# Normalised rows stored once, in the order in which the sequence transform reads them

## The chip, the cores and the metric

The kernel runs on one core of a Trainium2 chip. The metric is the device time of one execution in microseconds (us): 886.37 us before the change, the median of two runs (886.31 and 886.42).

## The reference

The input x has 2048 rows of 640 floats. Each row is normalised (mean and variance over its 640 values), and the output is the sum of x, a Fourier mixing of the normalised rows, and a two-layer network with a hidden width of 1536. Everything is float32.

```python
xn = layernorm(x)                                # no scale, no shift
a, b = xn @ dft_hid_re.T, xn @ dft_hid_im.T      # 640 x 640
y = dft_seq_re @ a - dft_seq_im @ b              # 2048 x 2048
h = gelu_tanh(xn @ w1 + b1)                      # 640 -> 1536
return x + y + (h @ w2 + b2)                     # 1536 -> 640
```

## The kernel before

Every matmul takes a float32 operand as two rounded halves ("high" on ACT, then "low" = value minus high on DVE, lines 187 and 190) and is done as three products (lines 312 to 314, or 332). So an operand is ready for PE only when an ACT and a DVE instruction have run for it, and both engines take their instructions strictly in the order of the program, as do the two queues that issue DMAs, SP and POOL. A DMA on SP also waits until the DMA issued eight places earlier on SP has landed, and POOL's DMAs likewise among themselves: each queue cycles through eight completion semaphores.

The rows are worked in four blocks of 512 rows (128 row chunks 0 to 15, four to a block). The program has these stages, all written out in one order by hand:

- **Block 0, the loop over i.** Block 0's hidden layer, twelve units of 128 columns: `hidden(g)` makes unit g (15 matmuls), `gelu` puts it through the activation and the split into `hs`, `output(g)` multiplies it into five PSUM banks. The weights come through `load_w1`, `load_w2` and are split by `prep_w1`, `prep_w2` three and one steps ahead. `background(i)` normalises the blocks 0, 1 ("a") and 2 ("b") meanwhile: `ln_stats` (two BN_STATS and a BN_AGGR a chunk), `ln_scale` (a square root on ACT, for which ACT changes its function table and back, and five tiny DVE instructions), `ln_apply` (one DVE instruction a chunk, in place). `put_z` regroups the normalised rows of a block into a tile `z` by 16 small DMAs on POOL, and `make_forms` transposes and splits `z` into the forms that the pairs stage multiplies. `z_a` goes into the tile `row`, and `z_b` into its own.
- **Pairs, k = 0 to 5.** The hidden layers of blocks 1 and 2 together. In each pair two units of block 1 (a1, a2) are used at once, and two of block 2 (b1, b2) are stored in DRAM (`keep`, tensor `gs`) and read back later. Units live in the two buffers `ab`; `zc` is a temporary in the buffers `zt`; `w2r` is a ring of three buffers. `beside_pair` adds block 0's sums to x (`finish`) and prepares the hidden transform's matrices.
- **Steps p = 0 to 13.** `output` of block 2's stored units, 15 matmuls a step. `between(p)` adds block 1's sums to x: `finish(1, e)` adds the bias on ACT, transposes bank e on DVE (line 395), and adds it on DVE to `xo[1]` (line 397), which is loaded from DRAM into the place `xab2` by four DMAs on SP (line 388). Block 2's sums use the banks 5, 6, 7, 3 and 4, so that step 2 needs the banks 3 and 4 of block 1 emptied. `between` also normalises block 3 and puts it into `z3`; from step 7 on `z3` is transposed and split for block 3's hidden layer, and the weights of that layer are split anew (`prep_w1`, loaded by `load_w1`).
- **Block 3, then the sequence transform.** Block 3's hidden layer runs beside `build`, which reads the normalised rows back from the DRAM tensor `xn`. The rest of the program, from about 350 us on, is the sequence transform.

The normalised rows go to DRAM twice: `put_rows(c)` stores a chunk in `xs` as it stands (four DMAs a block on POOL), and `by_chunks(t)` later copies a block from `xs` into `xn` in the order in which `build` reads it, by one DMA on SP inside DRAM.

Of the kernel before, what the change touches and what calls it, by code (L numbers as in the profile page):

```python
# [15 lines left out]
P = 128  # L16
# [10 lines left out]
def kernel(  # L27
# [66 lines left out]

    dram = ctx.enter_context(tc.tile_pool(name="dram", bufs=1, space=bass.MemoryType.DRAM))

    xs = dram.tile([S, D], F32, name="xs")
    xn = dram.tile([NS, P, D], F32, name="xn")

    gs = dram.tile([NF, P, TB], F32, name="gs")  # L100
# [98 lines left out]
    def rows_of(ap, t):  # L199
        return ap[t * TB : (t + 1) * TB].rearrange("(n r) d -> r n d", r=B)  # L200
# [29 lines left out]
    def ln_apply(c, eng=nc.vector, put=True):  # L230
        m = MV[:, slot[c]]
        eng.tensor_scalar(xt[c], xt[c], m[:, 0:1], m[:, 3:4], op0=ALU.subtract, op1=ALU.mult)  # L232
        if put:
            put_rows(c)

    def put_rows(c):
        nc.gpsimd.dma_start(xs[c * P : (c + 1) * P], xt[c])

    def ln_apply_chunked(dst, c, j0=0, j1=ND):

# [22 lines left out]
    def load_z(z, t):  # L263

        v = rows_of(xs, t)
        for q in range(Q):
            nc.gpsimd.dma_start(z[q * B : (q + 1) * B], v[:, :, q * DQ : (q + 1) * DQ])

    def transpose_z(key, z, j):
        zt[key] = mr.tile([P, TB], F32, tag="zt", bufs=2, name=f"zt{key}")  # L270
# [63 lines left out]
            )  # L334
        return acc

    def term(g, acc):

        a = mr.tile([P, TB], F32, tag="ab", bufs=2, name=f"ab{g}")
        nc.scalar.activation(a, acc, AF.Copy)  # L340
        return a

# [399 lines left out]
    def put_z(z, rows):  # L742

        for a in range(NC):
            for q in range(Q):
# [2 lines left out]
                    rows[a * B : (a + 1) * B, :, q * DQ : (q + 1) * DQ],  # L748
                )

    def background(i):

        if i == 0:
            for c in range(NC):
                ln_apply(c)
            A["rows_a"] = rows_in("rt2")
            for c in range(NC, 2 * NC):
                load_x(c, home=A["rows_a"])
            for c in range(2 * NC, 3 * NC):
                ln_stats(c)  # L760
        if i == 1:
            ln_scale(NC)
            Z["b"] = zo_tile("z_b")
            for c in range(2 * NC, 3 * NC):
                ln_apply(c, put=False)
            put_z(Z["b"], A["rows_b"])
            for c in range(2 * NC, 3 * NC):
                put_rows(c)
            ln_stats(NC)
            ln_stats(NC + 1)  # L770
        if i == 2:
            ln_stats(NC + 2)
            ln_stats(NC + 3)
            ln_scale(NC)
            Z["a"] = as_z(row_places)
            for c in range(NC, 2 * NC):
                ln_apply(c, put=False)
            put_z(Z["a"], A["rows_a"])
            for c in range(NC, 2 * NC):
                put_rows(c)  # L780
        if i == 4:
            open_place(*PLACES[7])
            new_forms(0, "vb", "ua", "va")
            make_forms("b", "vb0", "vb1", "ob0")
        if i == 5:
            make_forms("a", "ua0", "ua1", "va0")
        if i == 6:
            new_forms(3, "t1")
            make_forms("a", "oa0", "va1")
        if i >= 6:  # L790
            (ua, va), (ub, vb) = ((Z[k][:, :, : 2 * B], Z[k][:, :, 2 * B : 4 * B]) for k in "ab")
        if i == 6:
            add(ub, ub, ua, ALU.subtract)
        if i == 7:
            open_place(*PLACES[8])
            make_forms("b", "t10", "t11")
            add(vb, vb, ub, ALU.subtract)
        if i == 8:
            turn_x("t20", "b")
            turn_x("t21", "b")  # L800
            add(ua, vb, ua, ALU.subtract)
            add(va, va, vb, ALU.subtract)
            load_xo(0)


    XF = {}
# [96 lines left out]
        for e in es:  # L903
            add_block(xo[t], e, oacc[t][e], f"ot{t}_{e}", eng, bias=b2c[:, e : e + 1], **(home or {}))

    def by_chunks(t):

        nc.sync.dma_start(xn[:, t * B : (t + 1) * B], xs[t * TB : (t + 1) * TB].rearrange("(n r) d -> n r d", r=B))

    def store_sums(t, *ks):  # L910
        for k in ks or range(len(YCOLS)):
# [7 lines left out]
    def beside_pair(k, at):  # L919

        if k == 0:
            if at == 5:
                make_forms("a", "t30", "t31")
            if at == 6:
                make_forms("a", "t40", "t41")
                load_w(0, 0)
                load_w(1, 0)
            if at == 4:
                finish(0, 0, 1)
                store_sums(0, 0)  # L930
            return
        j = k - 1
        if k == 1:
            if at == 2:
                finish(0, 2, home=in_zt)
            if at == 5:
                finish(0, 3, home=in_zt)
                store_sums(0, 1)
                finish(0, 4)
                store_sums(0, 2)  # L940
        if at == 6:
            if k < NT:
                by_chunks(k - 1)
# [39 lines left out]
    def pair(k):  # L983
# [16 lines left out]
        beside_pair(k, 5)  # L1000
        put_out(0 if k else 3)
        window(x_, "C", 0, "t2", False)
        v = term(b1_, x_)
        beside_pair(k, 6)
        put_out(3 if k else 0)
        window(z_, "C", 2, "vb", False, ("C", 4, "ob0"))
# [21 lines left out]
    def between(p):  # L1028
# [2 lines left out]
            ln_stats(12)  # L1031
            ln_stats(13)
        if p == 1:
            finish(1, 3, 4, home=in_zt, eng=nc.vector)
            ln_stats(14)
        if p == 2:
            ln_stats(15)
            ln_scale(NC)
            Z["z"] = zo_tile("z3")
            for c in range(3 * NC, 4 * NC):  # L1040
                ln_apply(c, put=False)
            put_z(Z["z"], row_places)
            for c in range(3 * NC, 4 * NC):
                put_rows(c)
# [47 lines left out]
    for i in range(NF - 2):  # L1092
# [11 lines left out]
        gelu(i + 2, acc)  # L1104
        output(i)
    make_pieces(0, "Bh", "Bl", "+", "Dh", "Dl", "Ch", "Cl")
    split_x("t20")
# [570 lines left out]
```

## Time and profile before

| | |
|---|---|
| median of the runs | 886.37 us |
| the profiled execution, its own time | 887.41 us |
| its span, first to last instruction | 885.6 us |
| PE busy | 852.0 us, 96% of the span |
| DVE, ACT, POOL busy | 77%, 41%, 10% |
| mean granted TensorE clock | 0.986 |

Times below are microseconds from the start of the span. In a row of the timeline stand: start, length, engine, line, operation, tiles, shape, how many, and in brackets how long the engine had been idle before it and what ended that. In a row of waits stand: who waited, for what, the total, how many times, and the longest.

### The profile page before, as it was taken

To read this page: it belongs to the slowest core of one execution; us is meant where nothing else is said; L and a number is where in the kernel's file an instruction comes from. 1 tells how busy PE (TensorE), PEld (TensorE's weight loads), DVE (VectorE), ACT (ScalarE), POOL (GpSimd) and SP (SyncE) were. 2 spreads that over 40 slices of the span, in tenths; PEclk is the share of its full clock that TensorE was granted. 3 is DMA by queue.
4 is the path that set the end of the run, shared out by engine and by line. 5 is a ranking of instruction groups with operands and counts; after the bars stand their busy time and mean duration, and the time that the engine had idled before them with its cause. 6 is when DMAs were issued, how large, how long until landed. Compare 5 with 4: busy or idle time off the path is not lost.

```text
span 885.6 us, 10569 instructions
## 1 busy us (share of the span) xinstructions
PE 852.0 (96%) x3711; PEld 700.2 (79%) x3711; DVE 686.2 (77%) x897; ACT 367.3 (41%) x528; POOL 90.1 (10%) x142
## 2 busy tenths in 40 slices
PE   8997988999498999999999999999999999999997
PEld 7776877888386888888888888888888888888885
DVE  6859786876474377897989888888977988886587
ACT  6546554655144455543333444332222432323241
POOL 0370043333060500000000000000000000000000
PEclk9998999999699999999999999999999999999999
DMA  7893568988888787795964349947476679904364
GB/s 231 247 283 117 110 169 262 296 249 281 198 241 206 187 313 276 144 189 146 206 133 147 83 132 320 271 88 187 114 168 200 209 218 221 338 19 172 119 162 105
DMA packets 201188, 171.77 MB, mean 194 GB/s; under 512 B 65808, under 2 KB 172560, under 8 KB 200496
## 3 DMA queue, kind: packets, MB, share of 16 engines
q1 hardware_dynamic: 187168, 142.13, 60.5%
q0 software_dynamic: 8688, 28.06, 9.3%
q10 hardware_dynamic: 5280, 0.92, 0.5%
q8 instruction: 29, 0.48, 0.2%
q14 instruction: 23, 0.19, 0.1%
HBM read 120.99 MB, written 51.38 MB: 195 GB/s over the span
## 4 chain that ended last, share of the span: by engine, by line
PE 77%; DMA 7%; issue 6%; DVE 5%; ACT 1%; SPq 1%; POOL 1%; DVEq 0%; ACTq 0%; POOLq 0%
PE banks L312 24%; PE banks L313 24%; PE banks L314 24%; PE banks L332 5%; DMA w1r<-in_B_w_dram 2%; DMA z_b<-r 1%; DMA xab<-in_A_x_dram 1%; SPq L290 1%; POOL z L746 1%; DMA xs<-r 1%; DMA row<-rt 1%; DMA w2r<-in_B_w_dram 1%; DVE w1f L190 1%; DVE st L216 1%; DVE row L232 0%
## 5 line engine op out<-in xcount | busy, mean ns | idle before, releaser
L313 PE MATMUL banks<-as,xab 128*128 128x512 f32 x407 | 158.3, 389 | 0.0
L312 PE MATMUL banks<-as,xab 128*128 128x512 f32 x407 | 158.3, 389 | 0.0
L314 PE MATMUL banks<-as,xab 128*128 128x512 f32 x407 | 158.3, 389 | 0.0
L187 ACT ACTIVATE as<-r 128x1024 fp32r<-128x1024 f32 x80 | 85.0, 1062 | 173.6 <-PE banks L314 148.8
L190 DVE TENSOR_TENSOR as<-r,as 128x1024 fp32r<-128x1024 f32 x80 | 97.1, 1215 | 39.1 <-ACT as L187 39.1
L314 PEld LDWEIGHTS banks<-as,xab 128*128 128x128 f32 x407 | 76.4, 188 | 16.0
L313 PEld LDWEIGHTS banks<-as,xab 128*128 128x128 f32 x407 | 76.4, 188 | 15.9
L312 PEld LDWEIGHTS banks<-as,xab 128*128 128x128 f32 x407 | 76.4, 188 | 15.8
L312 PE MATMUL banks<-as,xc 128*128 128x512 f32 x224 | 87.1, 389 | 0.0
L313 PE MATMUL banks<-as,xc 128*128 128x512 f32 x224 | 87.1, 389 | 0.0
L314 PE MATMUL banks<-as,xc 128*128 128x512 f32 x224 | 87.1, 389 | 0.0
L187 ACT ACTIVATE as<-rt 128x1024 fp32r<-128x1024 f32 x32 | 34.0, 1063 | 69.8 <-PE banks L314 57.9
L312 PE MATMUL banks<-hs,xc 128*128 128x512 f32 x120 | 47.9, 399 | 12.9 <-DVE ot L395 12.9
L332 PE MATMUL banks<-xt,xab 128*128 128x512 f32 x240 | 57.6, 392 | 0.6 <-DVE xab L190 0.6
L190 DVE TENSOR_TENSOR hs<-ab,hs 128x512 fp32r<-128x512 f32 x36 | 26.3, 730 | 37.8 <-ACT hs L187 37.8
L332 PEld LDWEIGHTS banks<-xt,xab 128*128 128x128 f32 x240 | 44.6, 188 | 11.3 <-DVE xab L190 1.9
L314 PEld LDWEIGHTS banks<-as,xc 128*128 128x128 f32 x224 | 42.0, 188 | 8.8
L313 PEld LDWEIGHTS banks<-as,xc 128*128 128x128 f32 x224 | 42.0, 188 | 8.7
L312 PEld LDWEIGHTS banks<-as,xc 128*128 128x128 f32 x224 | 42.0, 188 | 8.7
L313 PE MATMUL banks<-hs,xc 128*128 128x512 f32 x120 | 47.7, 397 | 0.0
L314 PE MATMUL banks<-hs,xc 128*128 128x512 f32 x120 | 47.6, 397 | 0.0
L190 DVE TENSOR_TENSOR as<-rt,as 128x1024 fp32r<-128x1024 f32 x32 | 38.7, 1210 | 5.3 <-ACT as L187 5.3
(221 smaller groups left out, 1671.2 us busy)
## 6 DMA issues: line engine op xcount, KB each, us to landing
raw<-in_A_dft_seq_re_dram SPq DMA_DIRECT2D x64, 256.0 KB, 5.6
raw<-in_A_dft_seq_im_dram SPq DMA_DIRECT2D x64, 256.0 KB, 5.3
w1r<-in_B_w_dram SPq DMA_DIRECT2D x144, 80.0 KB, 3.1
wit<-wst POOLq DMA_DIRECT2D x15, 384.0 KB, 4.3
ws<-wit SPq DMA_DIRECT2D x15, 384.0 KB, 4.4
xn<-xs SPq DMA_DIRECT2D x4, 1280.0 KB, 7.6
wit<-wst POOLq DMA_DIRECT2D x20, 256.0 KB, 4.3
forms_ab<-xab SPq DMA_DIRECT2D x4, 1280.0 KB, 7.5
```

The lines of the kernel that those rows point to most:

```text
L187: nc.scalar.activation(h, s, AF.Copy)
L190: nc.vector.tensor_tensor(l, s, h.bitcast(F32), op=ALU.subtract)
L216: nc.vector.bn_stats(st[:, h, :], xt[c][:, h * half : (h + 1) * half])
L290: eng.dma_start(t[q * B : (q + 1) * B], v[q, :, :, f0 : f0 + P])
L312: nc.tensor.matmul(acc, wh, mh, start=first, stop=False, skip_group_check=goes_on)
L313: nc.tensor.matmul(acc, wh, ml, start=False, stop=False, skip_group_check=goes_on)
L314: nc.tensor.matmul(acc, wl, mh, start=False, stop=last, skip_group_check=goes_on)
L332: nc.tensor.matmul(acc, W1[i][:, a, j * P : (j + 1) * P], XT[j][:, b], start=n == 0, stop=n == len(steps) - 1)
L746: nc.gpsimd.dma_start(z[q * B : (q + 1) * B].rearrange("r (c a) d -> r a c d", a=NC)[:, a], rows[a * B : (a + 1) * B, :, q * DQ : (q + 1) ...
```

## The change

`xs` and the four copies inside DRAM are gone. `put_rows(t, rows)` stores a block straight into `xn`, by four DMAs of 32 partitions each. Block 2's four go out on SP, the others on POOL. `background` and the new `late` spread the row statistics and the square roots otherwise over the first steps; in `pair`, unit b1 gets a buffer of `w2r` (but in the last pair) and unit b2 is made in place in `zc`, so that neither is in `ab`; in `between`, the banks 3 and 4 of block 1 are transposed into `ab` in step 1 and added to `xo[1]` in step 4, and block 3 is normalised in step 3 instead of 2.

```diff
-    xs = dram.tile([S, D], F32, name="xs")
...
-    def put_rows(c):
-        nc.gpsimd.dma_start(xs[c * P : (c + 1) * P], xt[c])
...
-    def term(g, acc):
-        a = mr.tile([P, TB], F32, tag="ab", bufs=2, name=f"ab{g}")
+    def term(g, acc, a=None):
+        if a is None:
+            a = mr.tile([P, TB], F32, tag="ab", bufs=2, name=f"ab{g}")
...
+    def put_rows(t, rows, eng=nc.gpsimd):
+        for a in range(NC):
+            eng.dma_start(
+                xn[:, t * B : (t + 1) * B].rearrange("(c a) r d -> a r c d", a=NC)[a], rows[a * B : (a + 1) * B]
+            )
...
     def background(i):
         if i == 0:
             for c in range(NC):
                 ln_apply(c)
+            put_rows(0, row_places)
             A["rows_a"] = rows_in("rt2")
             for c in range(NC, 2 * NC):
                 load_x(c, home=A["rows_a"])
-            for c in range(2 * NC, 3 * NC):
-                ln_stats(c)
-        if i == 1:
-            ln_scale(NC)
-            Z["b"] = zo_tile("z_b")
-            for c in range(2 * NC, 3 * NC):
-                ln_apply(c, put=False)
-            put_z(Z["b"], A["rows_b"])
-            for c in range(2 * NC, 3 * NC):
-                put_rows(c)
-            ln_stats(NC)
-            ln_stats(NC + 1)
+            ln_stats(8)
+            ln_stats(9)
         if i == 2:
-            ln_stats(NC + 2)
-            ln_stats(NC + 3)
+            put_rows(2, A["rows_b"], nc.sync)
+            ln_stats(4)
+            ln_stats(5)
+        if i == 3:
             ln_scale(NC)
             Z["a"] = as_z(row_places)
             for c in range(NC, 2 * NC):
-                ln_apply(c, put=False)
+                ln_apply(c)
             put_z(Z["a"], A["rows_a"])
-            for c in range(NC, 2 * NC):
-                put_rows(c)
+            put_rows(1, A["rows_a"])
...
+    def late(i):                # called behind gelu(i + 2), ahead of output(i)
+        if i == 0:
+            ln_stats(10)
+            ln_stats(11)
+        if i == 1:
+            ln_scale(NC)
+            Z["b"] = zo_tile("z_b")
+            for c in range(2 * NC, 3 * NC):
+                ln_apply(c)
+            put_z(Z["b"], A["rows_b"])
+        if i == 2:
+            ln_stats(6)
+            ln_stats(7)
...
-    def by_chunks(t):
-        nc.sync.dma_start(xn[:, t * B : (t + 1) * B], xs[t * TB : (t + 1) * TB].rearrange("(n r) d -> n r d", r=B))
+    def turn_sum(t, e):
+        nc.scalar.activation(oacc[t][e], oacc[t][e], AF.Identity, bias=b2c[:, e : e + 1])
+        yt = mr.tile([P, TB], F32, tag="ab", bufs=2, name=f"ot{t}_{e}")
+        nc.vector.transpose(yt, oacc[t][e])
+        return yt
...
-        v = term(b1_, x_)
+        v = term(b1_, x_, None if k == LASTK else early.tile([P, TB], F32, tag="w2r", bufs=3, name=f"v{k}"))
...
-        keep(b2_, unit(b2_, x_, zc))
+        keep(b2_, unit(b2_, x_, zc, zc))
...
     def between(p):
         if p == 1:
-            finish(1, 3, 4, home=in_zt, eng=nc.vector)
+            held = [turn_sum(1, e) for e in (3, 4)]
+            A["held"] = held
             ln_stats(14)
         if p == 2:
             ln_stats(15)
+        if p == 3:
             ln_scale(NC)
             Z["z"] = zo_tile("z3")
             for c in range(3 * NC, 4 * NC):
-                ln_apply(c, put=False)
+                ln_apply(c)
             put_z(Z["z"], row_places)
-            for c in range(3 * NC, 4 * NC):
-                put_rows(c)
+            put_rows(3, row_places)
             new_xt(3)
+        if p == 4:
+            for e, yt in zip((3, 4), A["held"]):
+                d = xo[1][:, :, e * B : (e + 1) * B]
+                add(d, d, yt.rearrange("p (n i) -> p n i", i=B))
         if 4 <= p < 7:
-            finish(1, p - 4, eng=nc.vector)
-        if p == 5:
-            by_chunks(3)
+            finish(1, p - 4, home=in_zt, eng=nc.vector)
```

**The queues of the first 70 us.** On POOL stand, before, the stores of a block (line 237) and the 16 regrouping DMAs of a `z` (line 746) by turns; `row` holds block 0's rows and later `z_a`, `r` block 2's and `rt` block 1's.

```order
L237 DMA xs<-row 128x640 x4
L746 DMA z_b<-r_241 32x4x160 x16
L237 DMA xs<-r_241 128x640 x4
L746 DMA row<-rt_332 32x4x160 x16
L237 DMA xs<-rt_332 128x640 x4
L899 DMA gs<-ab_1028 128x512
L899 DMA gs<-ab_1064 128x512
```

In the changed kernel the same queue reads so (line 743 is the new store, 735 the regrouping, 902 `keep`):

```order
L743 DMA xn<-row 32x4x640 x4
L735 DMA z_b<-r_240 32x4x160 x16
L735 DMA row<-rt_331 32x4x160 x16
L743 DMA xn<-rt_331 32x4x640 x4
L902 DMA gs<-v_1027 128x512
L902 DMA gs<-zc_999 128x512
```

Block 2's store has left POOL from between the two regroupings. It stands on SP now, between the weight loads of the steps i = 2 and i = 3:

```order
L278 DMA w1r_460<-in_B_w_dram 32x5x128 x4
L285 DMA w2r_465<-in_B_w_dram 128x640
L743 DMA xn<-r_240 32x4x640 x4
L278 DMA w1r_522<-in_B_w_dram 32x5x128 x4
L285 DMA w2r_527<-in_B_w_dram 128x640
L278 DMA w1r_598<-in_B_w_dram 32x5x128 x4
```

The loads behind it on SP are moved back by four DMAs.

**DVE, the steps p = 1 and 2.** Before (`ot` is a transposed bank, `xab` here the place of `xo[1]`, `g` a stored unit read back, `row` block 3's rows):

```order
L190 TENSOR_TENSOR hs_2066<-g_1866,hs_2066 128x512
L395 STREAM_TRANSPOSE ot_3_2072<-banks 128x512
L397 TENSOR_TENSOR xab_2010<-xab_2010,ot_3_2072 128x16x32
L395 STREAM_TRANSPOSE ot_4_2076<-banks 128x512
L397 TENSOR_TENSOR xab_2010<-xab_2010,ot_4_2076 128x16x32
L216 BN_STATS st_91<-row 128x6 x2
L217 BN_AGGR mv<-st_91 128x2
L190 TENSOR_TENSOR hs_2097<-g_1868,hs_2097 128x512
```

In the changed kernel, the steps 1 to 3 on DVE begin so:

```order
L189 TENSOR_TENSOR hs_2056<-g_1857,hs_2056 128x512
L912 STREAM_TRANSPOSE ot_3_2062<-banks 128x512
L912 STREAM_TRANSPOSE ot_4_2065<-banks 128x512
L215 BN_STATS st_90<-row 128x6 x2
L216 BN_AGGR mv<-st_90 128x2
L189 TENSOR_TENSOR hs_2085<-g_1859,hs_2085 128x512
L215 BN_STATS st_91<-row 128x6 x2
L216 BN_AGGR mv<-st_91 128x2
L189 TENSOR_TENSOR hs_2108<-xab_1966,hs_2108 128x512
```

and the steps 3 and 4, behind the square root's five small instructions, go on so:

```order
L231 TENSOR_SCALAR row<-row,mv 128x640 x4
L189 TENSOR_TENSOR hs_2158<-xab_1966,hs_2158 128x512
L463 TENSOR_TENSOR xab_2000<-xab_2000,ot_3_2062 128x16x32
L463 TENSOR_TENSOR xab_2000<-xab_2000,ot_4_2065 128x16x32
L384 STREAM_TRANSPOSE ot_0_2164<-banks 128x512
L386 TENSOR_TENSOR xab_2000<-xab_2000,ot_0_2164 128x16x32
```

The addition of bank 3 no longer stands between the transposes of the banks 3 and 4; both additions come behind the normalisation of block 3 and the split of unit 28.

More of the change, by code (lines that the diff above doesn't have):

```diff
@@ L228, in ln_scale, with ln_apply @@
         nc.vector.scalar_tensor_tensor(r, t, 1.5, r, op0=ALU.add, op1=ALU.mult)
-    def ln_apply(c, eng=nc.vector, put=True):
+    def ln_apply(c, eng=nc.vector):
         m = MV[:, slot[c]]
         eng.tensor_scalar(xt[c], xt[c], m[:, 0:1], m[:, 3:4], op0=ALU.subtract, op1=ALU.mult)
-        if put:
-            put_rows(c)
-    def put_rows(c):
-        nc.gpsimd.dma_start(xs[c * P : (c + 1) * P], xt[c])
     def ln_apply_chunked(dst, c, j0=0, j1=ND):
@@ L261, in zo_tile @@
         return out_pool.tile(list(shape), dtype, tag="zo", bufs=1, name=name)
[L263 to L267, printed above, removed]
     def transpose_z(key, z, j):
@@ L941, in beside_pair @@
         if at == 6:
-            if k < NT:
-                by_chunks(k - 1)
             turn_w(0, j)
@@ L1040, in between @@
             for c in range(3 * NC, 4 * NC):
-                ln_apply(c, put=False)
+                ln_apply(c)
             put_z(Z["z"], row_places)
-            for c in range(3 * NC, 4 * NC):
-                put_rows(c)
+            put_rows(3, row_places)
             new_xt(3)
+        if p == 4:
+            for e, yt in zip((3, 4), A["held"]):
+                d = xo[1][:, :, e * B : (e + 1) * B]
+                add(d, d, yt.rearrange("p (n i) -> p n i", i=B))
         if 4 <= p < 7:
-            finish(1, p - 4, eng=nc.vector)
-        if p == 5:
-            by_chunks(3)
+            finish(1, p - 4, home=in_zt, eng=nc.vector)
         for j in {7: (0,), 8: (1, 2), 9: (3, 4)}.get(p, ()):
@@ L1104 @@
         gelu(i + 2, acc)
+        late(i)
         output(i)
```

## The prediction, as it was made before the changed kernel ran

> **What bounds the kernel now.** I read the page's shares first, then what PE waited for, then PE's timeline at each of those waits.
>
> ```profile
> PE 852.0 (96%) x3711; PEld 700.2 (79%) x3711; DVE 686.2 (77%) x897; ACT 367.3 (41%) x528; POOL 90.1 (10%) x142
> PEclk9998999999699999999999999999999999999999
> PE 77%; DMA 7%; issue 6%; DVE 5%; ACT 1%; SPq 1%; POOL 1%; DVEq 0%; ACTq 0%; POOLq 0%
> ```
>
> PE is the bound: 96% busy, and the chain that ended last is 77% PE. The 13% of DMA, "issue" and others in the chain is what a change of transfers and orders can reach; no matmul is taken away here. The waits of PE:
>
> ```profile
> PE banks L312 <- DVE ot L395: 12.9, 2, 11.2
> PE banks L332 <- ACT as L187: 4.6, 1, 4.6
> ```
>
> These are the two largest; the next two (on ACT's `hs` and `zc`) stand in brackets in the rows below. All four lie in the first 277 us, and behind them PE runs without a gap. A wait costs more than its length where the clock falls afterwards, so I price each place by the matmuls' starts:
>
> ```profile
> 67.68 0.39 PE L314 MATMUL banks<-hs,r 128*128 128x512 f32 x1
> 72.64 6.44 PE L332 MATMUL banks<-xt,as 128*128 128x512 f32 x15 [4.58 <-ACT as L187]
> 78.92 0.40 PE L312 MATMUL banks<-hs,r 128*128 128x512 f32 x1
> 82.33 3.56 PE L332 MATMUL banks<-xt,as 128*128 128x512 f32 x15
> 148.49 0.50 PE L312 MATMUL banks<-xab,w1f 128*128 128x512 f32 x1 [2.36 <-ACT zc L187]
> 225.52 0.39 PE L314 MATMUL banks<-hs,xc 128*128 128x512 f32 x1
> 237.09 0.79 PE L312 MATMUL banks<-hs,xc 128*128 128x512 f32 x1 [11.18 <-DVE ot L395]
> 242.37 0.42 PE L312 MATMUL banks<-hs,xc 128*128 128x512 f32 x1
> 267.37 0.39 PE L314 MATMUL banks<-hs,r 128*128 128x512 f32 x1
> 271.31 0.49 PE L312 MATMUL banks<-hs,rt 128*128 128x512 f32 x1 [3.55 <-ACT hs L187]
> 276.69 0.39 PE L313 MATMUL banks<-hs,rt 128*128 128x512 f32 x1
> ```
>
> At full clock the 15 matmuls from 78.92 to 82.33 take 3.41, 0.227 each. So: **A**, 67.68 to 78.92 holds 16 matmuls (3.63) and lasts 11.24: 7.6 lost. **B**, 225.52 to 242.37 holds 13 (2.95) and lasts 16.85: 13.9 lost. **C**, 267.37 to 276.69 holds 14 (3.18) and lasts 9.32: 6.1 lost. After 2.36 idle the next matmul is near its full speed (0.50 against 0.39); after 4.58, 15 of them take 6.44 instead of 3.56, so 2.9 of A's 7.6 is a slow clock, and after 3.55 there is a slow stretch too.
>
> [...]
>
> **B: the two banks, line by line.** Bank 3's addition waits on DVE for `xo[1]`, and bank 4's transpose stands behind it.
>
> ```profile
> 219.65 5.70 SPq L388 DMA_DIRECT2D xab<-in_A_x_dram  x4
> DMA to landing us min/median/max: 10.4/11.0/11.2
> 223.40 0.71 DVE L395 STREAM_TRANSPOSE ot<-banks 128x512 f32<-128x512 f32 x1
> 235.71 0.69 DVE L397 TENSOR_TENSOR xab<-xab,ot 128x512 f32<-128x512 f32 x1 [11.60 <-DMA w1r<-in_B_w_dram]
> 236.32 0.71 DVE L395 STREAM_TRANSPOSE ot<-banks 128x512 f32<-128x512 f32 x1
> 246.66 0.82 DVE L190 TENSOR_TENSOR xab<-w1r,xab 128x640 fp32r<-128x640 f32 x1
> ```
>
> The second line is of the four loads of `xo[1]`: the last, issued at about 224.4, lands at about 235.4, so I read the addition's wait as one for it, though the row names a weight load that landed beside it. With both transposes side by side bank 4 is empty at 223.40 + 2 x 0.71 = 224.8, ahead of PE, which asks for it at 225.52 + 0.23. All **13.9** goes.
>
> What is late next? With bank 4's three matmuls done at 226.4, PE's steps then begin at 226.4 + 3.41 x (p - 3). The additions still wait for 235.4, now in step 4, and queued behind them on DVE is the split of unit 29: 235.4 + two additions 1.38 + transpose 0.71 + addition 0.69 + a weight split 0.82 (last row) + the split itself 0.69 = 239.7. PE begins unit 29 (step 7) at 240.0 and reads the low half one matmul later. That just fits; each microsecond by which `xo[1]` comes later is paid from there on.
>
> **C: the copy on SP.** The weight loads of block 3 stand on SP behind `xn<-xs`, which waits for `xs` to land:
>
> ```profile
> SPq L908 <- DMA xs<-row: 9.3, 1, 9.3
> 259.35 11.73 SPq L290 DMA_DIRECT2D w1r<-in_B_w_dram  x12
> 270.00 0.74 ACT L187 ACTIVATE as<-w1r 128x640 fp32r<-128x640 f32 x1 [9.69 <-DMA w1r<-in_B_w_dram]
> ```
>
> ACT waits 9.7 for such a load at 270.00, the unit's split stands behind it, and PE pays 6.1. The copy is removed, so the loads go out when their buffers come free. But block 3's `z3` is made a step later, and PE arrives 14 sooner:
>
> ```profile
> 218.61 0.94 SPq L209 DMA_DIRECT2D row<-in_A_x_dram  x2
> DMA to landing us min/median/max: 4.9/6.9/10.0
> 239.27 0.88 DVE L216 BATCH_NORM_STATS2 st<-row 128x6 f32<-128x320 f32 x2
> 241.58 2.18 DVE L232 TENSOR_SCALAR row<-row,mv 128x640 f32<-128x640 f32 x4
> 255.47 1.30 DVE L271 STREAM_TRANSPOSE ztx<-z 128x512 f32<-128x512 f32 x2
> 258.32 0.69 DVE L190 TENSOR_TENSOR hs<-g,hs 128x512 fp32r<-128x512 f32 x1
> ```
>
> The last chunk of x lands at the latest at 219.0 + 10.0 = 229.0 (second line: the loads of block 3's chunks). From its statistics to the end of the normalisation were 243.76 - 239.27 = 4.5, and one unit's split (0.69) now stands between: 234.2. From there to the first transpose of `z3` 255.47 - 243.76 = 11.7: 245.9. Unit 32's split ended 3.5 behind that transpose: 249.4, and PE wants it in step 10, at 226.4 + 7 x 3.41 = 250.3. There is 0.9 to spare, and the next two units, each with two more transposes or splits ahead of it, have less. While `z3` comes in, four weight loads, the store of block 3's rows and that of block 1's sums share the engines with it. I take 1.2 for new waits here, from bounds of 0 and 6.1 (the wait as it was), nearer to nothing because the steps fit by the rows. C gives 6.1 - 1.2 = **4.9**.
>
> **A: `z_a` comes late.** ACT's weight split stands behind the forms of `z_a`, and these behind 16 DMAs on POOL.
>
> ```profile
> 34.48 2.18 DVE L232 TENSOR_SCALAR r<-r,mv 128x640 f32<-128x640 f32 x4
> 67.22 1.30 DVE L271 STREAM_TRANSPOSE ztua<-row 128x512 f32<-128x512 f32 x2 [7.86 <-DMA xs<-rt]
> 37.39 4.37 POOL L746 DMA_DIRECT2D z_b<-r  x8 [8.55 <-DVE r L232]
> 49.69 2.17 POOL L237 DMA_DIRECT2D xs<-r  x4 [1.42 <-DMA z_b<-r]
> 57.86 3.80 POOL L746 DMA_DIRECT2D row<-rt  x7 [0.41 <-DMA xs<-r]
> 62.35 1.09 POOL L746 DMA_DIRECT2D row<-rt  x2 [0.68 <-DMA row<-rt]
> ```
>
> With eight DMAs in flight at most, two halves of `z_b` take 49.69 - 37.39 = 12.3, or 6.15 a half. In the new order one more split (0.69) stands ahead of block 2's normalisation, so `z_b` starts at 38.1, and `z_a` can follow at 50.4, where `xs<-r` stood. Its second half goes out 6.15 later, at 56.5, the last of it at 56.5 + 7 x 0.55 = 60.4; before, the last went out at 62.9 and the transpose followed at 67.22, 4.3 later. So the transpose comes at 64.7, 2.5 sooner, and PE's matmuls at 70.1 instead of 72.64. PE has been ready since 67.9: 2.2 idle, and no slow stretch. At 70.1 + 3.41 = 73.5 it stands where it stood at 78.92: **5.4** gained. Bounds: all 7.6, and -0.7, where `z_a` lands no sooner for leaving POOL's line and the 0.69 is paid.
>
> A store of 32 partitions in 2560-byte pieces is in no row. The 128-partition store of the same bytes went from 49.69 to 57.86 (when POOL's wait for its last part ended): 8.2; the same bytes in `z_b`'s pieces of 640 took 12.3. I take the first, since its pieces are of 2560 bytes too; the other end and beyond is a rival below. On SP the four stand ahead of the weight loads from unit 9 on. Were these held until 57.86, as POOL was, they would still go out 12 before PE wants unit 9 at 70.1, so I cost that at nothing; without that cover, A's wait would be for the weights. The statistics and roots of blocks 1 and 2 are the same instructions in other places. What they delay on ACT and DVE are units that PE wants two steps later, 30 matmuls or 6.8 a step; if that cover is gone, `z_a` is later by as much, as with the 0.69.
>
> [...]
>
> ```profile
> q0 software_dynamic: 421, 0.92, 60.0%
> q1 hardware_dynamic: 673, 0.56, 44.0%
> ```
>
> **The pairs.** Unit a2 waited for the store of b1 to leave `ab`, and no longer does:
>
> ```profile
> ACT ab L351 <- DMA gs<-ab: 5.5, 2, 3.4
> ```
>
> The PE wait that follows is the 2.36 at 148.49. I take 0.7 of it, between nothing and 2.4, near nothing, because DVE's additions in that chain keep their places. The new places (`zc` held until its store lands, `w2r` used once more a pair) are reused a pair later, against waits of 3.4 at most for such a store; I cost them at nothing, and if that cover were gone it would be that wait again.
>
> **The sum.** 13.9 + 4.9 + 5.4 + 0.7 = 24.9 off the profiled execution's 887.41 is 862.5; the median of the runs lies 1.04 below that execution, so **861.5**. PE has no gap behind 277 us, and the engines' order is unchanged there, so nothing is given back.
>
> **The rivals.** *The engines are the limit* (0.22): with shares that sum to over 100%, `z_a` needs the same bytes moved as before, lands at 67.9, and A gives -0.7. The sum is 18.8, the time 867.6. Against it: the loads of SP that share the engines at that time are not wanted until later, and the store now stands among them. *The steps do not fit* (0.16): `z3`, `xo[1]` or the weight loads land 2 to 4 later when crowded into 14 fewer microseconds, and C keeps its 6.1 and B gives 10: 24.9 - 4.9 - 3.9 = 16.1, 870.3. *All waits go* (0.05): 30.0 off, 856.4. *Slower* (0.03): the 32-partition stores use the engines badly. Each block's store then adds d to the two regroupings in flight, `z_a` comes 2d later, and A's 5.4 turns into a loss of 2d - 5.4, with a slow clock's 2.9 on top. From d = 11 us, 1.31 MB in 19 instead of 8.2, the whole change is a loss (24.9 - 2 x 11 - 2.9 = 0); at d = 13 the time is 890. Against it: even the pieces of 640 bytes took 12.3. *It does not do what it says* falls away: the order has the transposes side by side and no copy. My forecast, 857 to 866, keeps 0.54.
>
> Range for 8 in 10: 856 to 872, from all waits gone to the steps not fitting with a little spread; without that rival too much would be left out. A change of 2%, 17.7 us, is about what a measurement of this kernel tells from none. Faster than 868.6 are the forecast (0.54), all waits gone (0.05), most of the engines' limit (0.16 of 0.22, as 867.6 is close to the mark) and a little of the steps (0.02): 0.77. Slower by that much is 0.02, the rest 0.21.
>
> **What would show it.** B: no wait of PE for a transposed bank, and DVE's wait for `xo[1]` moved behind block 3's normalisation. C: no ACT wait of 9 for a weight load; any wait of PE between 235 and 262 is the new one. A: the transpose of `z_a` at about 64.7 and the next 15 matmuls in 3.4; if it stays at 67, the engines were the limit. I am wrong if PE waits longer than 3.4 anywhere behind 80 us.

## The result, and the profile after the change

864.17 us, the median of two runs (863.83 and 864.51), against 886.37: a ratio of 0.975 with an interval of 0.9708 to 0.9792. Beside other kernels the changed one ran again, 866.60 in the median of three executions (865.85 to 866.72) against 888.82, a ratio of 0.9745 (0.9726 to 0.9763). A fourth of these executions, at 4900.77, stands outside everything and is not read. The kernel before took 888.2 to 888.8 in all later comparisons, so times are compared as ratios. The profiled execution took 864.51, 22.9 less than the one before; the spans, 862.5 and 885.6, differ by 23.1.

The shares and the chain on the page:

```profile
PE 846.3 (98%) x3711; PEld 696.1 (81%) x3711; DVE 686.9 (80%) x897; ACT 366.7 (43%) x528; POOL 87.2 (10%) x138
PE 74%; DMA 11%; DVE 6%; ACT 3%; SPq 2%; issue 2%; POOL 1%; POOLq 0%; DVEq 0%; ACTq 0%
```

The largest waits of PE, but for the first one of the span (total, times, longest):

```profile
PE banks L681 <- DVE xp L236: 2.2, 1, 2.2
PE banks L300 <- DVE ot L384: 2.2, 2, 1.7
PE banks L320 <- ACT as L186: 1.9, 2, 1.6
PE banks L300 <- ACT zc L186: 1.6, 2, 1.3
```

The work is the same (3711 matmuls); the waits of 12.9 for `ot` and 4.6 for `as` at the top of the list have become 2.2 and 1.9. Of the 12.9, 11.2 stood at B; the other 1.7, a wait for a transposed bank of block 0 in pair 1, was there before and is there after. Where the time came from is read by comparing the start of the same matmul in both traces:

| stretch | gained, us | the changed kernel is ahead by |
|---|---|---|
| start of the span to the first `output` (22.17, now 23.00) | -0.8 | -0.8 |
| to 54 us | 1.5 | 0.7 |
| place A (78.92, now 75.56) | 2.7 | 3.4 |
| pairs (148.49, now 143.50) | 1.6 | 5.0 |
| place B (242.37, now 223.43) | 13.9 | 18.9 |
| place C (276.69, now 252.31) | 5.4 | 24.4 |
| the rest, to the last matmul (879.46, now 856.46) | -1.4 | 23.0 |

The largest part, B's 13.9, comes from the order of the two transposes in step 1 and does not need the rows to be stored once; the new store bears on C and A.

**B.** PE's matmuls, then DVE:

```profile
220.48 0.39 PE L302 MATMUL banks<-hs,xc 128*128 128x512 f32 x1
220.71 0.39 PE L300 MATMUL banks<-hs,xc 128*128 128x512 f32 x1
218.31 1.31 DVE L912 STREAM_TRANSPOSE ot<-banks 128x512 f32<-128x512 f32 x2
229.72 1.29 DVE L463 TENSOR_TENSOR xab<-xab,ot 128x512 f32<-128x512 f32 x2 [0.71 <-DMA xab<-in_A_x_dram]
```

Where 11.57 lay between two matmuls there are now 0.23. Both transposes are done at 219.6, and the additions, 10 us later, wait 0.71 for `xo[1]`; the wait is on DVE still, where nothing hurries.

**C.** The transpose of `z3` on DVE, an ACT split that waits for its weights, and the two matmuls of PE that come late:

```profile
242.09 1.31 DVE L259 STREAM_TRANSPOSE ztx<-z 128x512 f32<-128x512 f32 x2 [3.00 <-DMA xn<-row]
254.46 0.74 ACT L186 ACTIVATE as<-w1r 128x640 fp32r<-128x640 f32 x1 [2.62 <-DMA w1r<-in_B_w_dram]
245.61 0.50 PE L301 MATMUL banks<-hs,r 128*128 128x512 f32 x1
249.46 0.50 PE L301 MATMUL banks<-hs,rt 128*128 128x512 f32 x1
```

No copy stands ahead of the weight loads; ACT waits 2.6 for them where it waited 9.7, and PE doesn't feel it. The two matmuls begin 0.42 and 0.54 behind the ones ahead of them (245.19 and 248.92) instead of 0.23: 0.5 lost, where 6.1 were.

**A.** DVE's first transposes of `z_b` and of `z_a`, PE's matmuls of the units 8 and 9, and POOL's issues of `z_a`:

```profile
56.71 1.30 DVE L259 STREAM_TRANSPOSE ztvb<-z_b 128x512 f32<-128x512 f32 x2 [6.59 <-DMA row<-rt]
66.18 1.30 DVE L259 STREAM_TRANSPOSE ztua<-row 128x512 f32<-128x512 f32 x2 [2.51 <-DMA row<-rt]
62.14 5.70 PE L320 MATMUL banks<-xt,as 128*128 128x512 f32 x15 [1.57 <-ACT as L186]
71.62 4.10 PE L320 MATMUL banks<-xt,as 128*128 128x512 f32 x15 [0.37 <-ACT as L186]
50.91 1.64 POOL L735 DMA_DIRECT2D row<-rt  x3 [1.53 <-DMA z_b<-r]
56.24 3.80 POOL L735 DMA_DIRECT2D row<-rt  x7 [1.31 <-DMA z_b<-r]
63.10 0.55 POOL L735 DMA_DIRECT2D row<-rt  x1 [0.23 <-DMA row<-rt]
```

One wait has become two. `z_a` is 1.0 sooner than before (67.22), but `z_b` is 4.8 later (51.92), so that unit 8, which did not wait before, now waits 1.57 and runs its 15 matmuls at a slow clock (5.70 instead of 3.56; granted clock 0.50 from 64 to 66). POOL begins `z_a` at 50.91, but still waits for a piece of `z_b` to land at 56.24, and issues the last piece at 63.10.

### The profile page after: what moved, and what is told of

The parts are those of the page before. It is cut to its first block, busy times and chain, and to the rows that moved or that the text cites. A ratio compares the mean times of both kernels' runs of the same rounds, so it can differ in the third digit from the quotient of the medians.

```text
span 862.5 us, 10569 instructions
## 1 busy us (share of the span) xinstructions
PE 846.3 (98%) x3711; PEld 696.1 (81%) x3711; DVE 686.9 (80%) x897; ACT 366.7 (43%) x528; POOL 87.2 (10%) x138
## 4 chain that ended last, share of the span: by engine, by line
PE 74%; DMA 11%; DVE 6%; ACT 3%; SPq 2%; issue 2%; POOL 1%; POOLq 0%; DVEq 0%; ACTq 0%
PE banks L300 24%; PE banks L301 24%; PE banks L302 24%; PE banks L320 3%; DMA w1r<-in_B_w_dram 2%; DMA row<-xn 2%; DMA z_b<-r 2%; DMA xab<-in_A_x_dram 1%; DMA ys<-xo 1%; SPq L278 1%; DVE xab L463 1%; DMA row<-rt 1%; DVE sums L463 1%; POOL xo L386 1%; DVE w1f L189 1%
## 5 line engine op out<-in xcount | busy, mean ns | idle before, releaser
L320 PE MATMUL banks<-xt,xab 128*128 128x512 f32 x240 | 56.7, 390 | 0.0
L300 PE MATMUL banks<-hs,xc 128*128 128x512 f32 x120 | 46.9, 391 | 2.2 <-DVE ot L384 2.2
L301 PE MATMUL banks<-hs,xc 128*128 128x512 f32 x120 | 46.7, 389 | 0.0
L302 PE MATMUL banks<-hs,xc 128*128 128x512 f32 x120 | 46.7, 389 | 0.0
```

The lines of the kernel that those rows point to most:

```text
L300: nc.tensor.matmul(acc, wh, mh, start=first, stop=False, skip_group_check=goes_on)
L301: nc.tensor.matmul(acc, wh, ml, start=False, stop=False, skip_group_check=goes_on)
L302: nc.tensor.matmul(acc, wl, mh, start=False, stop=last, skip_group_check=goes_on)
L320: nc.tensor.matmul(acc, W1[i][:, a, j * P : (j + 1) * P], XT[j][:, b], start=n == 0, stop=n == len(steps) - 1)
```

## The experiments

### What the place A hangs on: block 2's store

Four kernels move or change that store alone (in *last*, block 2's rows are missing from `xn`).

```diff
 (later)    put_rows(2, A["rows_b"], nc.sync)   from step i = 2 to i = 3
 (last)     removed; behind put_rows(1, ...): put_rows(2, A["rows_a"])      on POOL
 (pool)     removed; behind put_z(Z["b"], ...): put_rows(2, A["rows_b"])    on POOL
 (128)      nc.sync.dma_start(xs[c * P : (c + 1) * P], xt[c]) for c = 8..11, and in pair 3
            nc.sync.dma_start(xn[:, 2 * B : 3 * B], xs[2 * TB : 3 * TB] ...)
```

Later:

> The changed kernel with block 2's store one step later on SP, behind the weight loads of the step i = 3. Theory (the 16 DMA engines are full from 36 to 70 us, so that what is put ahead delays what stands behind, and z_a lands when all bytes ahead of it have been moved): z_b is transposed at about 52.5 instead of 56.71, and the matmuls of unit 8 begin without a wait at about 60.4 instead of 62.14; z_a stays at 66.2 within 0.7, PE now waits about 4 us at once for unit 9's weights and gets a slow clock of about 2.9 behind it. Time 866.7 (changed kernel 864.2). Rival (POOL's queue holds z_a, not the engines): with z_b sooner, z_a follows sooner too, at 62 to 64, and the wait for unit 9 is under 1 us: 861 to 862.

Last:

> The changed kernel with block 2's store taken from SP; behind block 1's store POOL stores the same bytes once more, but out of block 1's rows, so block 2's rows are missing from the sequence transform's input. Nothing but weights stands beside z_b and z_a. Theory (full engines): z_b at about 52.5, z_a 4.7 us sooner than in the changed kernel (1.31 MB at the 278 GB/s of that stretch), at 61.5; both waits of PE there, 3.9 and 1.1 us with their slow clock, go but for 0.5 at most: 859.5. Rival (the weight loads, not the store, hold back z_b and z_a): z_b stays at 56, z_a at 65 or later, time within 1 us of 864.

Pool:

> The changed kernel with block 2's store on POOL between the two regroupings, where it stood before the change. Theory (full engines): z_b at about 52.5 and z_a at 66 to 67, as before the change; the wait for unit 9 is 4 to 4.6 us with a slow clock of 2.9: 867 to 867.5. Rival (the prediction's: leaving POOL's line makes z_a 2.5 us sooner): z_a comes 2.5 us later than in the changed kernel, at 68.7, and PE pays for all of it: 869.5 or more.

128:

> The changed kernel with block 2's store at the same place on SP, but as four DMAs of 128 partitions into the tensor xs, and one copy inside DRAM in pair k = 3, as before the change, for this block alone. Theory (only the bytes count): z_b and z_a within 0.7 of 56.71 and 66.18, time within 1 us of 864.2. Rival (stores of 32 partitions use the engines badly): z_b 2 us or more sooner, time 862 or less.

Measured (transposes in the profiled execution, PE's loss from 60 to 80 us, ratio to the kernel before; the changed kernel in its first and second profile):

| kernel | `z_b` | `z_a` | PE loses | ratio (interval) |
|---|---|---|---|---|
| before | 51.92 | 67.22 | 7.6 | 1 |
| changed | 56.71; 54.72 | 66.18; 66.03 | 4.9; 7.4 | 0.975; 0.9745 |
| later | 54.13 | 63.04 | 1.5 | 0.974 (0.9721 to 0.976) |
| last | 55.19 | 63.63 | 2.1 | 0.9715 (0.9696 to 0.9734) |
| pool | 55.64 | 68.67 | 9.8 | 0.9778 (0.9754 to 0.9803) |
| 128 | 55.55 | 65.94 | 6.5 | 0.9746 (0.9728 to 0.9763) |

*Pool* is the clear one: the price that the rival put on it, 2.5 us for `z_a`, came out as 2.6 and 2.5. In the rows of POOL and DVE of that kernel

```profile
59.83 5.42 POOL L735 DMA_DIRECT2D row<-rt  x10 [1.00 <-DMA xn<-r]
68.67 1.31 DVE L259 STREAM_TRANSPOSE ztua<-row 128x512 f32<-128x512 f32 x2 [6.06 <-DMA xn<-rt]
```

the last ten regrouping DMAs go out only when a piece of the store has landed: POOL's line does hold `z_a`. (The time of *pool*, 868.84, stayed a little under the 869.5 that the rival gave.) My theory for these runs, that the engines alone decide, fell here. *Later* says the same: its `z_a` came at 63.04, as the rival had it. Its other three executions took 864.3 to 866.1 where the profiled one took 860.9, so it is no faster version.

In *last* both were partly wrong. `z_b` should have come at 52.5 without the store, and came at 55.19. SP shows why the store's absence freed little:

```profile
44.32 2.29 SPq L278 DMA_DIRECT2D w1r<-in_B_w_dram  x4
47.21 0.35 SPq L285 DMA_DIRECT2D w2r<-in_B_w_dram  x1
```

Where the store stood, the weight loads move up (47.75 in the changed kernel). The time of *last* does not show A alone, since its profile lost 3.6 in the steps, to small waits and a slow clock behind them (matmuls 0.43 apart from 245.46 to 248.45 instead of 0.23), where the changed kernel's lost 0.5. *128* moves neither `z_b` nor `z_a` nor the time by more than the changed kernel's two profiles differ: for block 2's store, 128 partitions or 32 make no difference here.

### How far executions spread, and B and C undone and alone

> The changed kernel once more, beside the other three on the same chip, to see how far single executions of it spread. Theory: the landing of z_b and z_a differs from execution to execution, as the four kernels so far spread over 2 to 5 us each where the traces before 55 us and behind 76 us are alike; so 862 to 867, with the same waits behind 76 us (pairs 3.7, the steps about 0.5). Rival: the spread comes from the steps or the end, and the place A (60 to 76 us) loses 4.9 again within 0.3.

The changed kernel itself took 866.60, inside the 862 to 867 expected. Its losses behind 76 us were those of the first profile within 1 us (pairs 3.7, steps 1.5 instead of 0.5), and A's was 7.4 instead of 4.9. Five profiles share the changed code up to 79 us (the two above, B undone, and the two of the pairs further down): `z_b` at 54.3 to 56.7, `z_a` at 65.1 to 66.3, and PE loses 4.7 to 7.4. The code before has two profiles, its own and that of B alone: `z_b` at 51.92 and 50.00, `z_a` at 67.22 and 67.30, and PE loses 7.6 and 8.1. So A is what spreads most, and with it the time by some 2.5 us.

B alone, on the kernel before:

```diff
-            finish(1, 3, 4, home=in_zt, eng=nc.vector)
+            A["held"] = [turn_sum(1, e) for e in (3, 4)]
+        if p == 4: (both additions to xo[1], as in the changed kernel)
```

> The kernel before with B's edit alone: the banks 3 and 4 turned into ab in step 1, added in step 4; rows still go through xs and a copy on SP in step 5. Theory (B and C are one chain): PE comes to C's place 13.9 sooner, block 3's normalisation about 9.6 sooner (234.2 instead of 243.8), so the copy on SP and the weight loads behind it come 9.5 sooner too, the first split at about 260.5, while PE wants it at 253.5: C's loss grows from 6.1 to about 10.9, and the kernel gains 13.9 - 4.8 = 9.1 on the kernel before. First rival (C keeps its size): 13.9 gained. Second rival (the copy does not move, since it waits on something else): C's loss grows by all of 13.9, and nothing is gained.

880.96 against 888.82: 0.991 (0.9894 to 0.9926), 7.9 gained. PE's wait for the banks is gone, and at C it waits so:

```profile
PE banks L312 <- ACT hs L187: 8.0, 1, 8.0
```

Behind that wait stand, on SP and ACT:

```profile
250.76 0.54 SPq L908 DMA_DIRECT2D xn<-xs  x1
261.95 0.74 ACT L187 ACTIVATE as<-w1r 128x640 fp32r<-128x640 f32 x1 [10.47 <-DMA w1r<-in_B_w_dram]
```

With the slow clock behind it (matmuls 0.43 apart from 264.79 to 269.06) C loses 11.4 instead of 6.1. The copy came at 250.8 (9.5 sooner than before would have been 249.2) and the split at 262.0 (260.5 expected). In this profile a wait of 2.25 in pair 1 also brought a slow clock of 1.4 (matmuls 0.43 apart from 150.33 to 153.31), which the kernel before did not pay for its 2.36 (granted clock 1.00 from 148 to 152). B and C are one chain: whoever had made B's edit alone would have seen 8 of its 13.9.

C undone, on the changed kernel (stores into `xs`, copies by SP as before the change), and B undone:

```diff
+            nc.sync.dma_start(xn[:, t * B : (t + 1) * B], xs[t * TB : (t + 1) * TB] ...)   # pairs 1 to 3, step 5
```
```diff
-            held = [turn_sum(1, e) for e in (3, 4)]
+            finish(1, 3, 4, home=in_zt, eng=nc.vector)
```

> The changed kernel with the rows stored in xs (four DMAs of 128 partitions a block, at the same places) and copied into xn inside DRAM by one DMA of SP a block, in pairs 1 to 3 and step 5, as before the change. Theory: the copy of block 3 waits on SP for block 3's store, which stands behind z3's 16 DMAs, and the weight loads wait behind it, now that PE comes 13.9 sooner: C loses about 10.9 instead of 0.5, 10 above the changed kernel. First rival (C as it was before the change, 6.1): 5.6 above. Second rival (the copies of the pairs cost as well): more than 12 above, with waits of PE in pairs 1 to 3.

> The changed kernel with B's edit undone: bank 3 is transposed and added, then bank 4, in step 1. Theory: DVE's addition waits for xo[1] again (landing at about 229.5 at the latest) with bank 4's transpose behind it; PE loses 11 to 14 there and nothing is given back later, since no load waits for a copy: 11 to 14 above the changed kernel. Rival (the new order around it hides part of the wait): less than 8 above it.

C undone took 874.51, 0.9842 (0.9818 to 0.9866); B undone 874.85, 0.984 (0.982 to 0.9859): about 8 above the changed kernel each. PE's wait with C undone, and SP and ACT behind it:

```profile
PE banks L301 <- ACT hs L187: 9.0, 1, 9.0
```
```profile
241.69 0.55 SPq L915 DMA_DIRECT2D xn<-xs  x1
252.95 0.74 ACT L187 ACTIVATE as<-w1r 128x640 fp32r<-128x640 f32 x1 [10.12 <-DMA w1r<-in_B_w_dram]
```

PE's wait with B undone, and DVE behind it:

```profile
PE banks L300 <- DVE ot L384: 13.3, 2, 11.6
```
```profile
230.70 0.69 DVE L386 TENSOR_TENSOR xab<-xab,ot 128x512 f32<-128x512 f32 x1 [12.08 <-DMA xab<-in_A_x_dram]
```

Both mechanisms came back at their place and size: 11.2 lost at C (10.9 expected), 13.3 at B (11 to 14). (In the row of B undone 11.6 of the waits are B's and 1.7 are those in pair 1; B's 13.3 is read from the matmuls' starts and holds a slow clock of 1.7 behind the wait, with matmuls 0.43 apart from 232.67 to 234.80.) The times rose by less. With B undone the profiled executions, 866.60 and 875.19, differ by 8.6: B's 13.3, less 2.8 because A lost 4.7 instead of 7.4, less 1.8 because PE comes later to the next steps and their small waits go. With C undone A itself was better in the profile (1.5 lost), which leads to the next point.

### What stays open at A

C undone differs from the changed kernel, ahead of 60 us, only in the form of the stores. The DMAs from 24 to 37 us (packets and rate; then KB each and the median time to landing), in the changed kernel:

```profile
DMA packets 2780, 3.11 MB, mean 239 GB/s; under 512 B 800, under 2 KB 2080, under 8 KB 2779
xn<-row POOLq DMA_DIRECT2D x4, 320.0 KB, 5.8
rt<-in_A_x_dram SPq DMA_DIRECT2D x4, 320.0 KB, 8.3
```

and with C undone:

```profile
DMA packets 2887, 3.77 MB, mean 290 GB/s; under 512 B 645, under 2 KB 1930, under 8 KB 2887
xs<-row POOLq DMA_DIRECT2D x4, 320.0 KB, 4.8
rt<-in_A_x_dram SPq DMA_DIRECT2D x4, 320.0 KB, 5.1
```

With block 0's store in the new form the engines move 232 to 247 GB/s in that stretch in ten profiles and 258 in the eleventh (*later*), with the old form 263, 290 and 296 in three; and in C undone `z_b` came at 52.96 and `z_a` at 62.70. This points to block 0's store of 32 partitions as a part of what makes `z_b` late. It is not shown: no run changed that store alone, and the other executions of C undone were 3.6 to 6.4 slower than the profiled one. The other candidate is SP's traffic beside the second half of `z_b`: SP issued no load from 42.6 to 47.8 before the change, and in every kernel with the new stores it issues a store or weight loads then. But C undone, with the old form, does so too, nearly without a break from 41.1 to 49.7, and its `z_b` came sooner than any with the new form (54.13 at best), so this traffic alone does not account for the delay. How much is whose stays open.

### The statistics, another queue, the pairs

Statistics, roots and normalisations in their old places (`late` emptied into `background`, the stores as changed):

> The changed kernel with the statistics, roots and normalisations of the blocks 1 and 2 in their old places (block 2's statistics in step 0, its normalisation and block 1's first statistics in step 1 ahead of the unit, block 1's normalisation in step 2); the stores stay as changed. Theory (the new places free DVE, so that PE loses nothing between 30 and 54 us, at the price of the weight loads going out sooner, in z_b's time): PE loses 1.1 to 1.5 again between 30 and 54; z_b is transposed 1 to 3 us sooner than in the changed kernel (54.7 to 56.7). Its gain and loss nearly cancel: time within 1.5 us of the changed kernel, 864 to 867. Rival (the places matter only for DVE): the 1.1 to 1.5 come back and z_b stays: 1 to 1.5 above the changed kernel; or they do nothing: no loss between 30 and 54.

```profile
42.24 4.59 PE L320 MATMUL banks<-xt,xab 128*128 128x512 f32 x13 [1.89 <-DVE xab L189]
```

866.61, 0.9758 (0.9736 to 0.9779): no difference from the changed kernel. PE lost 3.7 between 39 and 47, more than before the change; half of it is a slow clock behind the wait of 1.89 (13 matmuls in 4.59 instead of 3.1). `z_b` stayed at 56.57, so my theory of the sooner weight loads got no support, and `z_a` came at 67.54; PE lost nothing at unit 8 and 4.4 at unit 9. What the new places save early is waited away at A, since `z_a` sets the end of both.

Half of `z_a`'s DMAs issued by ACT:

```diff
-                nc.gpsimd.dma_start(
+                (nc.gpsimd if a < 2 else nc.scalar).dma_start(      # for z_a
```

> The changed kernel with the second half of z_a's 16 DMAs issued by ACT (idle there from 47.8 to 57.5 in the changed kernel) instead of POOL: the same bytes, another queue. Theory (POOL's line of eight in flight and 0.55 an issue is what holds z_a, since the store put back on POOL made it 2.5 later): z_a is transposed at 60 to 61.5 instead of 66.0, the wait for unit 9 goes, the one for unit 8 (z_b) stays: 861 to 863. Rival (the engines are full, so another queue brings nothing): z_a at 65 to 66, time within 1 us of the changed kernel's 864 to 867.

```profile
47.57 8.92 ACTq L735 DMA_DIRECT2D row<-rt  x8
44.45 11.94 SPq L743 DMA_DIRECT2D xn<-r  x4
59.84 6.42 PE L320 MATMUL banks<-xt,xab 128*128 128x512 f32 x15 [6.75 <-ACT xab L186]
```

867.34, 0.9769 (0.9751 to 0.9787). Neither happened: eight issues held ACT for 8.92, and four on SP beside them took 11.94 instead of 3.50; ACT's splits stood behind, and PE lost 9.7 a unit earlier. When `z_a` itself landed can't be read from it, because DVE came to the transpose late (68.24).

The units of the pairs back in `ab`:

```diff
-        v = term(b1_, x_, None if k == LASTK else early.tile(... tag="w2r" ...))
+        v = term(b1_, x_)
-        keep(b2_, unit(b2_, x_, zc, zc))
+        keep(b2_, unit(b2_, x_, zc))
```

> The changed kernel with units b1 and b2 of the pairs made in ab, as before the change. Theory: unit a2 of pair 1 waits again some 3.4 us for the store of b1 to leave ab, and PE's waits at 120.2 and 141.8 in pair 1 grow from 0.37 and 1.50 to 0.97 and 2.52: 1.6 above the changed kernel, 866 to 868. Rival (the places cost as much in the w2r ring or in zc as they save in ab): within 0.3 of it, and the waits of pair 1 stay.

```profile
ACT ab L340 <- DMA gs<-ab: 5.2, 2, 3.2
```

867.88, 0.9784 (0.9752 to 0.9816). The wait of 5.5 before the change is back (in the changed kernel there is none), and PE's losses in pair 1 grew by 0.5 and 0.8, the second with a slow clock of 1.5 behind it (matmuls 0.43 apart from 147.37 to 150.35): 2.8 at its place, 1.6 expected. The interval overlaps with the changed kernel's; it is the trace that shows the gain, not the time.

A version that might have been better, with ACT's copy of `z_`'s bank ahead of unit a1's activation, and in pair 1 the transposes of block 0's banks 3 and 4 ahead of the weight pieces:

```diff
+        high(zc, z_)
         u = unit(a1, y_, u, u)
-        split_unit(a1, u, lambda _: high(zc, z_))
+        split_unit(a1, u)
-        make_pieces(k + 1, "+"); beside_pair(k, 5)
+        beside_pair(k, 5); make_pieces(k + 1, "+")      # k = 1
```

> The changed kernel with two things moved in the pairs: ACT copies z_'s bank into zc ahead of unit a1's activation, and in pair 1 DVE transposes block 0's banks 3 and 4 ahead of the sums of the weight pieces. Theory (each of the three waits of PE left in pair 1 is an instruction standing behind another that it doesn't need, as B's was): the losses at 120.2, 122.8 and 141.8 (0.37, 1.86, 1.50, the same in every run so far but the one with the pairs undone) go to 0.5 in all, and nothing is late behind them: 3.2 below the changed kernel's 864.2 to 866.7, so 861 to 863.5, 0.970 to 0.971 of the kernel before. Rival (what is moved back becomes late: unit a1's halves, or the weight pieces): a new wait of PE of 1 to 3 us between 125 and 150, and the time stays within 1 us of the changed kernel.

867.66, 0.9777 (0.9747 to 0.9807): not faster. The three old waits went to 0.3, and three new ones came:

```profile
PE banks L300 <- DVE zc L463: 4.6, 3, 2.0
```

Pair 0 shows how, on ACT and DVE:

```profile
102.16 0.60 ACT L186 ACTIVATE zc<-banks 128x512 f32<-128x512 f32 x1 [3.47 <-PE banks L302]
104.07 0.69 DVE L189 TENSOR_TENSOR hs<-ab,hs 128x512 fp32r<-128x512 f32 x1 [4.03 <-ACT hs L186]
```

ACT now waits for `z_`'s matmuls ahead of the activation; DVE waits for its `hs`, and the sum for unit b2, which PE waits for, stands behind that on DVE. The rival was right.

## Why the prediction was right, point by point

861.5 was forecast and 864.17 measured, inside 856 to 872; in the profiled executions 22.9 came of 24.9. The mechanisms at B and C are as forecast. That the sum comes so close is partly luck: 2.7 less than forecast at A and 2.1 lost at places costed at nothing stand against 2.9 more than forecast in the pairs, at C and ahead of 54 us. The sign of being wrong, a wait of PE over 3.4 behind 80 us, did not come; the longest is 1.70. No run shows 3.4 as the length from which the clock falls: behind the 1.57 at unit 8, 15 matmuls took 5.70, and behind the 2.36 before the change there was no slow stretch. So the 2.2 at A, costed without one, could have had one.

- **B**, 13.9 forecast: 13.9 measured, and 13.3 when undone. That the addition waited for `xo[1]`, though the row named a weight load, is now shown by name (B undone: 12.08 for `xab<-in_A_x_dram`). The additions moved to step 4 made nothing late.
- **C**, 4.9 forecast: 5.4 measured. The rival that the steps don't fit did not come. New waits cost 0.5 here, not 1.2, but that is a good execution: in the ten profiles with the changed steps and block 3's changed store these waits, with the slow clock behind them, cost 0.2 to 3.6, in the median 1.1, so the 1.2 was a fair size. `z3`'s first transpose was due 20.4 behind PE's arrival at bank 4 (225.5 to 245.9) and came 21.6 behind it (220.48 to 242.09).
- **Pairs**, 0.7 forecast: 1.6. ACT's wait for the store was worth 1.0 of the 2.36 that follows it, and 0.6 of another that I had not priced: ACT's chain in pair 1 came sooner as a whole.
- **A**, 5.4 forecast: 2.7, and in other executions 0.2 to 3.4 (losses of 4.7 to 7.4 against 7.6 and 8.1 in the two profiles of the code before). This is the step that failed. The queue was right: leaving POOL's line is worth 2.5 to 2.6 to `z_a`. What failed was that `z_b`'s halves would take 6.15 each as before, so that `z_a` could start at 50.4 and be transposed at 64.7, and PE could stand at 73.5 (75.56 measured) where it had stood at 78.92. `z_a` started at 50.9, but its last DMA went out at 63.1 instead of 60.4, because `z_b`'s pieces landed later. And I looked at unit 9 alone: `z_b` had been in time by so much that I did not see that unit 8 hangs on it. The rival of the engines had `z_a` at 67.9, and was off as well; the shares that it starts from, 60.0% and 44.0%, are those of two DMA queues from 55 to 60 us before the change. In *pool* the store held back the last ten regrouping DMAs of its queue.
- **Statistics and roots**, costed at nothing: 1.5 gained ahead of 54 us. Undoing them brings 3.7 back there and no time at the end.
- **"Nothing is given back" behind 277 us**: 1.3 was, in two waits on DVE of 0.45 (at 272) and 0.34 (at 355), each with a slower matmul behind it (0.50 instead of 0.39). The start of the span cost another 0.8, which I had not priced: the first normalisation (`xp`) held PE for 2.2 instead of 0.7. In other executions of the changed code it was 0.5 to 2.6, so this is spread and not the change.
- **32-partition stores**, the slower rival: not at d = 11. The store from SP lands at 7.2 us where the old one from POOL took 5.7; a part of A's missing 2.7 may be theirs, as said above.

## What to carry to other kernels

Two waits in one chain are priced together: with the first gone, the engine arrives sooner at the second, and what it waits for may not move (B alone gave 8 of 13.9, B with C 19.3). When a transfer leaves a crowded queue, ask what moves up into its place, and look at every consumer of that stretch, also those that were in time. An instruction moved ahead in an in-order queue takes its own wait along, and all behind it then wait too (in the reordered pairs DVE waited 4.03 for ACT's `hs`, and PE 4.6 in three waits for `zc`); B's edit worked because the transposes waited for nothing.

## What the runs showed of the hardware that I had not expected

In these runs a wait's length alone did not decide whether the clock fell behind it. Unit 8 waited 1.57 in the changed kernel, and its 15 matmuls took 5.70 (row at A above); with B undone it waited 1.47, and they took 4.14:

```profile
61.86 4.14 PE L320 MATMUL banks<-xt,as 128*128 128x512 f32 x15 [1.47 <-ACT as L186]
```

The stretch from 64 to 66 us of the changed kernel (busy time of PE, PEld, DVE, ACT, POOL; granted clock; DMA share; GB/s):

```profile
64.00:66.00 2.00, 2.00 (x6) 1.57 (x5) 0.00 (x0) 0.00 (x0) 1.70 (x4) 0.50 0.81 203
```

The first ran at half the clock there, the second at the full one (granted clock 1.00 from 64 to 66); the wait of 2.36 before the change did not slow either, and that of 2.25 at the same place in B alone did. In *last* even 1.10, with another 0.44 behind the next matmul, put the next matmuls 0.43 apart from 245.46 to 248.45, where 0.23 is full clock. So the 2.36 and the 3.55 of the kernel before do not enclose a length from which the clock falls: 1.57 was enough. What decides besides the length is not shown.

A subtraction on DVE took longer beside an addition on POOL. One of 128x640 took 0.81 at 148.70, with POOL idle, and 2.26 at 127.34, beside an addition on POOL (rows of the changed kernel; the kernel before has the same pair, 0.80 at 153.70 and 2.27 at 131.31):

```profile
127.34 2.26 DVE L189 TENSOR_TENSOR w1f<-w1r,w1f 128x640 fp32r<-128x640 f32 x1
127.53 1.38 POOL L386 TENSOR_TENSOR xo<-xo,ot 128x512 f32<-128x512 f32 x1
148.70 0.81 DVE L189 TENSOR_TENSOR w1f<-w1r,w1f 128x640 fp32r<-128x640 f32 x1
```

Why is not shown. This slowing is a part of why the reordered pairs failed: the sums of the weight pieces, moved beside POOL's additions, took 2.71 where two of them had taken 0.89, and only a part of that came back, as the subtraction of 2.26 stood clear of POOL there and took 0.81.
